# Talking-heads attention, top-1 experts and a dense layer on one core: tokens numbered by partition and tile, one store for the gates, and the low parts of turned operands moved ahead of the maximum

## The chip, the core and the metric

The kernel runs on one core of a Trainium2 chip. The engines of that core named here are TensorE (PE; its weight loads are listed as PEld), VectorE (DVE), ScalarE (ACT), GpSimd (POOL) and SyncE (SP). Each runs its own list of instructions in order and waits at semaphores for the others. Transfers between DRAM and on-chip memory (SBUF) are started from the lists of SP, ACT and POOL and are carried by 16 DMA engines that they share. Matrix products land in PSUM, eight banks of 128 partitions.

The metric is the time of one execution in microseconds of device time. Runs are given as median, lowest and highest. One further execution is taken with a profiler; rows of profile and trace come from that one.

## The reference

Three stages follow one another; the result of each is the input of the next.

```python
# q, k, v: (4, 12, 448, 64)   w_pre, w_post: (12, 12)
scores = scale * q @ k.T                      # per batch and head
scores = einsum('bhij,hg->bgij', scores, w_pre)
attn = exp(scores - max(scores)); attn = attn / (sum(attn) + 1e-09)
attn = einsum('bhij,hg->bgij', attn, w_post)
x = (attn @ v), heads side by side            # (1792, 768)

# experts: emb (8, 768), w1 (8, 768, 1024), w2 (8, 1024, 768)
logits = normalized(x) @ normalized(emb).T / tau
expert_idx = argmax(logits)
gate_w = softmax(logits)[expert_idx]
x = gate_w * (relu(x @ w1[expert_idx]) @ w2[expert_idx])

# dense: w_in (768, 2048), w_out (2048, 768)
h = x @ w_in
out = (h - tanh(h)) @ w_out
```

All inputs and the output are float32. w_in and w_out come as 64-bit floats and are converted on the chip.

## The kernel before

**Precision.** Most products are formed from a high part and a low part of each operand: the high part is the operand copied to a shorter float format (by ScalarE), the low part is the operand minus the high part (by VectorE or POOL). Three products, high by high, low by high and high by low, are summed in PSUM.

**Attention.** Each batch's 448 query rows are cut in four tiles of 120, 120, 120 and 88 rows, 16 tiles T in all (`IT`). A tile is worked in blocks of 10 rows of all 12 heads, so that (row, head) pairs lie on 120 partitions. There are 180 blocks (`NBK`), one for each step of a loop written at lines 1127 to 1160. Step s forms P(s), the product of the rows of S with w_pre (`emit_P`, line 386); VectorE takes the maximum of P from PSUM, ScalarE exponentiates, VectorE makes the weights w from the sum (`emit_W`, lines 402 to 405), and two steps later (`LAG`) TensorE forms T from p and w and ScalarE copies T out (`emit_TE`). The rows of S come from SBUF by a DMA on SP (`emit_relay`), started up to seven steps ahead.

Between these the steps carry the work of other tiles: q and k are turned by TensorE (`tr_q`, `tr_k`) for a later tile, S is formed for the next tile (`emit_S`, `emit_S2`), and A·V and X for an earlier one (`emit_AV2`, `emit_X`). A table (`side`, filled by `at` and `at_e`) says in which step each stands. A turned operand lies in the one PSUM bank with tag e until both its parts are taken: the high part by ScalarE (`flush`, at the start of the next step) and then the low part by VectorE (`flush2`, line 1138, behind `emit_P` and `emit_W` of that step). The next transpose, the second half of `emit_S2` and `emit_X` write the same bank.

The row order inside a block is r, r + nb, r + 2·nb and so on, so position p of a tile is not token p of the tile. The kernel corrects that where rows leave the chip: `x_store` (line 470) writes x to `x_d` in token order through a view of 12 by 10 (or 8 by 10) rows, and the remaining 8 rows of an 88-row tile by a second DMA. `tokf` holds the token number of each place.

**Routing.** `emit_R` ranks the tokens of each expert and makes `ids`, the token numbers of the slots of each expert. Rows of x are then gathered by these numbers from DRAM (`gather`, POOL). The gates, 128 by 16 numbers, are computed in pieces in the first expert (`emit_G`, a generator that `pump(5)` advances after each chunk), written to `gate_d` in token order by 20 DMAs on SP, and gathered again by the same numbers (`gates`, POOL).

**Experts.** Items 0 to 6, an item for overflow rows, and 7 follow one another. An item has eight chunks of h and eight parts of y. During the parts of y of item n the weights of item n+1 are split in high and low parts (`do1`); each split frees one of four buffers, and the load of a later weight is put on SP's queue at that place (`feed1`, `feed2`). At the same place in item 0 the rows of item 1 are multiplied by their gates (line 700) and turned (`xsplit`, line 705). Results go to `yT` in slot order; `sid_d` holds the token number of each slot.

**Dense layer.** Two halves of 896 slots by eight groups g of 256 columns; `stageA` forms h and the activation, `stageB` the product with w_out, one round later. At j = 2 SP loads the token numbers of all slots to `sid`; at the last group of a half POOL scatters the finished rows to the output by them (line 1377).

The scheduler keeps the order that the code is written in, and a DMA on SP or ACT also waits for the DMA eight places before it in a ring of eight semaphores.

Of the kernel before, what the change touches and what calls it, by code (L numbers as in the profile page):

```python
# [9 lines left out]
F32 = mybir.dt.float32  # L10
# [3 lines left out]
I32 = mybir.dt.int32  # L14
# [17 lines left out]
def body(ctx: ExitStack, tc, q, k, v, w_pre, w_post, emb, tau, w1, w2, win, wout, out):  # L32
# [3 lines left out]
    NT = B * S  # L36
# [32 lines left out]
        psum.append(ctx.enter_context(tc.tile_pool(name="psum3", bufs=1, space=PSUM, reuse_waits="tile")))  # L69
        PB.append({"h": 3, "o": 5})  # L70

    x_d = dram.tile([NT, DM], F32, name="x_d")
    NOV = 12
    NTP = NT + CAP
    sid_d = dram.tile([NTP, 1], I32, name="sid_d")
    gate_d = dram.tile([NT, 1], F32, name="gate_d")
    wi_d = dram.tile([DM, F2], F32, name="wi_d")
    wo_d = dram.tile([F2, DM], F32, name="wo_d")

# [58 lines left out]
    if True:  # L138
# [64 lines left out]
        pool.affine_select(tri, tri, pattern=[[1, 128]], compare_op=ALU.is_gt, fill=0.0, base=0, channel_multiplier=-1)  # L203
        revi = cp.tile([128, E], F32, name="revi")
        pool.iota(revi, pattern=[[-1, E]], base=E, channel_multiplier=0, allow_small_or_imprecise_dtypes=True)

        rk = cp.tile([128, 12], F32, name="rk")
        pool.iota(rk[:, 0:11], pattern=[[-10, 11]], base=-10, channel_multiplier=1, allow_small_or_imprecise_dtypes=True)
# [11 lines left out]
        dve.tensor_add(rq[:, 3:4], rq[:, 3:4], rq[:, 5:6])  # L220
        rowf = cp.tile([128, B, 4], F32, name="rowf")
        pool.iota(rowf, pattern=[[S, B], [120, 4]], base=0, channel_multiplier=0, allow_small_or_imprecise_dtypes=True)
        rg4 = tokf.rearrange("p (b t) -> p b t", b=B)
        dve.tensor_scalar(rg4[:, :, 0:3], rowf[:, :, 0:3], rq[:, 1:2], None, ALU.add)
        dve.tensor_scalar(rg4[:, :, 3], rowf[:, :, 3], rq[:, 3:4], None, ALU.add)
        dve.tensor_copy(tokh, tokf)
        pool.iota(iota_s, pattern=[[1, CAP]], base=0, channel_multiplier=0, allow_small_or_imprecise_dtypes=True)

        valid = cp.tile([128, 4], F32, name="valid")
# [156 lines left out]
        def emit_P(i):  # L386
            n = 12 * blocks[i][2]
            t = sr.pop(i)
            pt = ps("b", f"P{i}")
            pe.matmul(pt[:n, :S], wpre[:n, :n], t[:n, :], start=True, stop=True)  # L390
            mx = a2.tile([120, 4], F32, tag="mx", name=f"mx{i}", bufs=5)
            dve.tensor_reduce(mx[:n, 0:1], pt[:n, :S], op=ALU.max, axis=AX.X, negate=True)  # L392
            p = a2.tile([120, S], F32, tag="p", name=f"p{i}", bufs=LAG + 1)
            pj[i] = (p, mx)
            return lambda: act.activation(p[:n, :], pt[:n, :S], AF.Exp, bias=mx[:n, 0:1], scale=1.0, accum_out=mx[:n, 1:2])  # L395
# [72 lines left out]
        xms = {}  # L468

        def x_store(eng, T, xm, cs):  # L470

            b, it = divmod(T, 4)
            i0, n = IT[it]
            r0, nb = b * S + i0, n // 10
            eng.dma_start(x_d[r0:r0 + 10 * nb, cs].rearrange("(m r) d -> r m d", r=nb), xm[:10 * nb, cs])
            if n % 10:
                eng.dma_start(x_d[r0 + 10 * nb:r0 + n, cs], xm[10 * nb:n, cs])

        def emit_X(T, hf, cpy=act.copy):
            b, it = divmod(T, 4)  # L480
# [95 lines left out]
        def emit_G():  # L576
            yield
            bc = lambda t: t.rearrange("p (t o) -> p t o", o=1).to_broadcast([128, 4 * B, E])
            for rn in inv_norm(ssk, 128, 4 * B, "r"):
                yield  # L580
            dve.tensor_sub(lk, lk, bc(mxk))
            yield
            dve.tensor_mul(lk, lk, bc(rn))
            act.activation(lk, lk, AF.Exp)
            yield
            es = small([128, 4 * B], F32, "es")
            dve.reduce_sum(es, lk, axis=AX.X)
            yield
            dve.tensor_scalar_add(es, es, 1e-9)
            yield  # L590
            dve.reciprocal(gate, es)
            yield
            yield

            gvs = dram_disjoint_views(gate_d, 5 * B)
            for T in range(4 * B):
                bq, it = divmod(T, 4)
                i0, n = IT[it]
                r0, nb = bq * S + i0, n // 10
                sp.dma_start(gvs[T][r0:r0 + 10 * nb].rearrange("(m r) o -> r (m o)", r=nb), gate[:10 * nb, T:T + 1])  # L600
                if n % 10:
                    sp.dma_start(gvs[4 * B + bq][r0 + 10 * nb:r0 + n], gate[10 * nb:n, T:T + 1])
                if T % 4 == 3:
                    yield

        def emit_ov():

# [52 lines left out]
    with mctx:  # L660
# [358 lines left out]
        for T in range(4 * B - 1):  # L1019
# [7 lines left out]
            for gi, (_, t1) in enumerate(RG[:-1]):  # L1027
                if t1 == T + 1:
                    for x, y in enumerate((0, 2, 2, 4, 4)):
                        at(e + 5 + y, emit_R, gi, x)  # L1030
        CA = CONV_A
        for j in range(CA):
            st = 12 + (NBK - 24) * j // CA
            at(st - 4, conv_load, j, ap)
            at(st, conv_do, j, ap)
# [41 lines left out]
        def flush2(tag=None):  # L1077
            for x in late2[:]:
                if tag in (None, x[0]):
                    late2.remove(x)  # L1080
                    x[1]()
# [45 lines left out]
        for s in range(NBK + LAG + 6):  # L1127
            todo = side.get(s, [])
            fill = [x for x in todo if x[0] in PEF]
            for fn, a in todo:  # L1130
                if fn in (load_q, load_k, load_v, conv_load):
                    fn(*a)
            flush()
            relay_to(s + NSR - 1)
            ex = emit_P(s) if s < NBK else lambda: None
            if 0 <= s - 1 < NBK:
                emit_W(s - 1)
            flush2()
            for fn, a in todo:
                if fn is emit_R and a[1] in (0, 1, 3):  # L1140
                    fn(*a)
# [120 lines left out]
    with ExitStack() as dctx:  # L1262
# [25 lines left out]
        def wi_load(g, eng=sp):  # L1288
            r = raw6
            eng.dma_start(r, wi_d[:, g * GF * 128:(g + 1) * GF * 128].rearrange("(c p) f -> p c f", p=128))  # L1290
            return r
# [105 lines left out]
        for j, (hf, g) in enumerate(seq):  # L1397
            nx = seq[j + 1][1] if j + 1 < len(seq) else None
            if nx is not None and j:
                wr = wi_load(nx)  # L1400
            if j == 2:
                sp.dma_start(sid, sid_d[0:NT].rearrange("(t p) o -> p (t o)", p=128))

            groups = [(t, nh) for t in range(HT // 128) for nh in range(2)] if prev is not None else []
            work = []
# [72 lines left out]
```

## Time and profile before

| | us |
|---|---|
| median of 3 runs | 1436.76 |
| lowest, highest | 1435.28, 1438.02 |
| the profiled execution | 1437.55 |
| its span, first to last instruction | 1435.8 |
| PE busy in the span | 1317.8 (92%) |
| DVE, ACT, POOL busy | 1030.4 (72%), 751.2 (52%), 531.4 (37%) |

The stages by the time from the span's start: attention steps from 22.9 to about 533 us, the experts from 557 to about 943, the dense layer from there to the end. The mean granted clock of TensorE is 0.97 of full speed.

In the rows further down, "idle before" is the time for which an engine did nothing ahead of an instruction, and the name behind the arrow is what ended that time. Tile names have their numbers left out: P is the score after w_pre, ptk and ptq are turned k and q in PSUM, kh and kl, qh and ql their high and low parts, xgi a gathered block of x, w1hi and w1li the parts of a weight, r a weight as loaded. SPq and ACTq rows are the issuing of DMAs.

### The profile page before, as it was taken

How to read it: one execution, taken by the hardware profiler on the slowest of the kernel's cores; microseconds unless marked ns; L12 is line 12 of the kernel's file. 1: busy time of each engine (PE TensorE's matmuls, PEld its weight loads, DVE VectorE, ACT ScalarE, POOL GpSimd, SP SyncE). 2: the span in 40 equal slices, each digit the busy share in tenths (PEclk: the TensorE clock that was granted, in tenths of full speed). 3: DMA queues.
4: the chain of work that ended last, by engine and by line, in shares of the span. 5: the costliest groups of instructions: out<-in, count | busy, mean ns of one | idle time of the engine just before them, and what ended most of it. 6: DMA issues, size and time to landing. Idle time of an engine off the chain costs nothing. (4 is left out here: it accounts for less than half of the span.)

```text
span 1435.8 us, 25691 instructions
## 1 busy us (share of the span) xinstructions
PE 1317.8 (92%) x9426; PEld 1152.5 (80%) x9426; DVE 1030.4 (72%) x2178; ACT 751.2 (52%) x1515; POOL 531.4 (37%) x528
## 2 busy tenths in 40 slices
PE   8989998999899986488999997969999999999998
PEld 5766776776677766488999996959999998999997
DVE  5766776667667664367777775468888799888886
ACT  6766666665666654224444445256444455544441
POOL 0222322232223223143455442335444446544433
PEclk9999999999999998789999998988999999999999
DMA  5655565556456464458787775222112113122101
GB/s 159 196 154 153 183 191 139 158 185 191 129 170 199 141 206 142 80 169 202 250 252 235 222 219 170 67 67 67 45 44 67 54 57 121 45 67 67 45 23 77
DMA packets 147563, 194.06 MB, mean 135 GB/s; under 512 B 59595, under 2 KB 111227, under 8 KB 147435
## 3 DMA queue, kind: packets, MB, share of 16 engines
q1 hardware_dynamic: 140539, 177.29, 41.9%
q0 software_dynamic: 3024, 12.20, 2.3%
q10 hardware_dynamic: 3872, 2.90, 0.7%
q8 instruction: 76, 1.25, 0.4%
q14 instruction: 52, 0.43, 0.1%
HBM read 130.21 MB, written 23.61 MB: 107 GB/s over the span
## 5 line engine op out<-in xcount | busy, mean ns | idle before, releaser
L427 PEld LDWEIGHTS T<-w,p 120*112 120x112 f32 (+1 forms) x1440 | 165.9, 177 | 65.5 <-issue 49.2
L133 POOL TENSOR_TENSOR cm<-cm,ct 128x256 f32<-128x256 f32 x96 | 73.5, 765 | 335.0 <-DVE ct L130 298.3
L427 PE MATMUL T<-w,p 120*112 120x120 f32 (+1 forms) x1440 | 184.9, 272 | 5.3 <-DVE w L405 3.0
L392 DVE TENSOR_REDUCE mx<-P 120x1 f32<-120x448 f32 x180 | 111.9, 622 | 97.9 <-PE P L390 96.8
L390 PE MATMUL P<-sr,wpre 120*120 120x448 f32 x360 | 166.5, 544 | 1.0 <-DMA sr<-ssb 0.9
L395 ACT ACTIVATE p<-P,mx 120x448 f32<-120x448 f32 x180 | 113.8, 632 | 97.1 <-DVE mx L402 86.1
L1317 POOL TENSOR_TENSOR gl<-th,gh 128x448 fp32r<-128x448 f32 x64 | 74.8, 1169 | 239.3 <-ACT gh L1316 192.7
L1331 PE MATMUL h<-yh,wih 128*128 128x448 f32 x384 | 142.7, 372 | 11.1 <-ACT yh L1279 9.2
L1368 PE MATMUL o<-woh,gh 128*128 128x384 f32 x448 | 150.7, 336 | 1.8 <-DVE acc L1374 1.8
L1369 PE MATMUL o<-wol,gh 128*128 128x384 f32 x448 | 150.8, 337 | 0.0
L1370 PE MATMUL o<-woh,gl 128*128 128x384 f32 x448 | 150.7, 336 | 0.0
L1333 PE MATMUL h<-yh,wil 128*128 128x448 f32 x384 | 143.2, 373 | 3.1 <-POOL wil L1306 3.1
L1332 PE MATMUL h<-yT,wih 128*128 128x448 f32 x384 | 142.7, 372 | 0.4 <-DVE yT L1280 0.4
L1374 DVE TENSOR_TENSOR acc<-acc,o 128x384 f32<-128x384 f32 x196 | 106.5, 547 | 45.6 <-PE o L1370 45.1
L1337 ACT ACTIVATE u<-h 128x448 f32<-128x448 f32 x64 | 34.9, 545 | 183.8 <-PE h L1333 183.8
L785 PE MATMUL hi<-xhi,w1hi 128*128 128x256 f32 x384 | 111.5, 290 | 15.4 <-DVE hli L789 15.2
L432 ACT COPY A<-T 112x480 f32<-112x480 f32 x180 | 101.2, 562 | 21.9 <-PE T L427 21.5
L727 PE MATMUL ypi<-hhi,w2hi 128*128 128x256 f32 x384 | 111.9, 291 | 0.0
L729 PE MATMUL ypi<-hhi,w2li 128*128 128x256 f32 x384 | 110.0, 286 | 0.0
L786 PE MATMUL hi<-xli,w1hi 128*128 128x256 f32 x384 | 109.9, 286 | 0.0
L728 PE MATMUL ypi<-hli,w2hi 128*128 128x256 f32 x384 | 109.8, 286 | 0.0
L787 PE MATMUL hi<-xhi,w1li 128*128 128x256 f32 x384 | 109.5, 285 | 0.0
(259 smaller groups left out, 3398.2 us busy)
## 6 DMA issues: line engine op xcount, KB each, us to landing
sr<-ssb SPq DMA_DIRECT2D x176, 210.0 KB
r<-in_moe_w SPq DMA_DIRECT2D x72, 384.0 KB
r<-in_moe_w SPq DMA_DIRECT2D x52, 512.0 KB
craw<-in_moe_w_in SPq DMA_DIRECT2D x48, 256.0 KB
craw<-in_moe_w_out SPq DMA_DIRECT2D x48, 256.0 KB
raw<-wi_d SPq DMA_DIRECT2D x15, 768.0 KB
wor<-wo_d SPq DMA_DIRECT2D x15, 768.0 KB
wi_d<-cm SPq DMA_DIRECT2D x48, 128.0 KB
```

What stands on the lines that cost most here:

```text
L390: pe.matmul(pt[:n, :S], wpre[:n, :n], t[:n, :], start=True, stop=True)
L392: dve.tensor_reduce(mx[:n, 0:1], pt[:n, :S], op=ALU.max, axis=AX.X, negate=True)
L395: return lambda: act.activation(p[:n, :], pt[:n, :S], AF.Exp, bias=mx[:n, 0:1], scale=1.0, accum_out=mx[:n, 1:2])
L427: pe.matmul(pt[:CP, c * n:(c + 1) * n] if m == 10 else pv[:, c], p[:n, c * CP:(c + 1) * CP], w[:n, :] if m == 10 else wv, start=True, stop ...
L727: pe.matmul(o, wh[:, sl], a, start=False, stop=False)
L785: pe.matmul(pt[:, :256], wh[:, sl], xh[:, c, :], start=c == 0, stop=False)
L1331: pe.matmul(pt[:, :S], wi[0][:, c, sl], yh[:, c, :], start=c == 0, stop=False)
L1332: pe.matmul(pt[:, :S], wi[0][:, c, sl], yl[:, c, :], start=False, stop=False)
L1333: pe.matmul(pt[:, :S], wi[1][:, c, sl], yh[:, c, :], start=False, stop=c == KD - 1)
L1368: pe.matmul(pt[:, :384], gh[:, sl], wo[0][:, f, n0:n0 + 384], start=f == 0, stop=False)
L1369: pe.matmul(pt[:, :384], gh[:, sl], wo[1][:, f, n0:n0 + 384], start=False, stop=False)
L1370: pe.matmul(pt[:, :384], gl[:, sl], wo[0][:, f, n0:n0 + 384], start=False, stop=f == GF - 1)
```

## The change

Tokens are numbered p·16 + T by partition p and tile T, which needs 2048 numbers for 1792 tokens. `x_d` and `gate_d` have 2048 rows in this numbering, `tokf` is an iota, and each store of x is one DMA with one row for each partition. The 256 rows that belong to no token are written with zeros by five DMAs in step 8, and a table `row_d` from number to token row by a sixth. All gates are stored by one DMA on ACT's queue, 64 bytes for each partition. In the dense layer the numbers of the slots go to `sidc`, and POOL looks the token rows up in `row_d` by 14 gathers at j = 3 to 7. And `flush2`, the low parts, is called inside `emit_P`, behind the product and ahead of the maximum.

```diff
+    NC = 128 * 4 * B
+    x_d = dram.tile([NC, DM], F32, name="x_d")
+    row_d = dram.tile([NC, 1], I32, name="row_d")
...
+        pool.iota(tokf, pattern=[[1, 4 * B]], base=0, channel_multiplier=4 * B, allow_small_or_imprecise_dtypes=True)
+        dve.tensor_copy(tokh, tokf)
...
+        def store_rows():
+            zr = xbuf[1]
+            dve.memset(zr, 0.0)
+            xv = x_d.rearrange("(p t) d -> t p d", t=4 * B)
+            sp.dma_start(x_d[NC - 128:NC, :], zr)
+            for b in range(B):
+                sp.dma_start(xv[4 * b + 3, 88:120, :], zr[:32])
+            sp.dma_start(row_d.rearrange("(p t) o -> p (t o)", t=4 * B), rowi)
...
             pe.matmul(pt[:n, :S], wpre[:n, :n], t[:n, :], start=True, stop=True)
+
+            flush2()
             mx = a2.tile([120, 4], F32, tag="mx", name=f"mx{i}", bufs=5)
...
-            eng.dma_start(x_d[r0:r0 + 10 * nb, cs].rearrange("(m r) d -> r m d", r=nb), xm[:10 * nb, cs])
-            if n % 10:
-                eng.dma_start(x_d[r0 + 10 * nb:r0 + n, cs], xm[10 * nb:n, cs])
+            n = IT[T % 4][1]
+            eng.dma_start(x_d.rearrange("(p t) d -> t p d", t=4 * B)[T, :n, cs], xm[:n, cs])
...
-            for T in range(4 * B):
...
-                sp.dma_start(gvs[T][r0:r0 + 10 * nb].rearrange("(m r) o -> r (m o)", r=nb), gate[:10 * nb, T:T + 1])
-                if n % 10:
-                    sp.dma_start(gvs[4 * B + bq][r0 + 10 * nb:r0 + n], gate[10 * nb:n, T:T + 1])
-                if T % 4 == 3:
-                    yield
+            act.dma_start(gate_d.rearrange("(p t) o -> p (t o)", t=4 * B), gate)
+            yield
...
+        at(8, store_rows)
...
-            flush2()
...
+            if 2 < j < 8:
+                for k in range(3 * (j - 3), min(NT // 128, 3 * (j - 2))):
+                    pool.indirect_dma_start(out=sid[:, k:k + 1], out_offset=None, in_=row_d,
+                                            in_offset=bass.IndirectOffsetOnAxis(ap=sidc[:, k:k + 1], axis=0))
             if j == 2:
-                sp.dma_start(sid, sid_d[0:NT].rearrange("(t p) o -> p (t o)", p=128))
+                sidc = dp.tile([128, NT // 128], I32, name="sidc")
+                sp.dma_start(sidc, sid_d[0:NT].rearrange("(t p) o -> p (t o)", p=128))
```

Three places show what stands where. VectorE in attention step 28, before: mx is the maximum of P and, in the next three rows, the steps to the weights w of the block before; kl1_3 is the low part of turned k (batch 1, pair 3), lg a small sum of X.

```order
L392 TENSOR_REDUCE mx28_1283<-P28_1281 120x1
L402 TENSOR_SCALAR mx27_1237<-mx27_1237 120x1
L403 RECIPROCAL mx27_1237<-mx27_1237 120x1
L405 TENSOR_SCALAR w27_1288<-wpost_130,mx27_1237 120x120
L311 TENSOR_TENSOR kl1_3_1277<-ptk1_3_1271,kh1_3_1276 128x448
L493 TENSOR_REDUCE lg_174<-X0_0_1298 120x8
```

The same place in the changed kernel:

```order
L325 TENSOR_TENSOR kl1_3_1287<-ptk1_3_1281,kh1_3_1286 128x448
L408 TENSOR_REDUCE mx28_1294<-P28_1291 120x1
L418 TENSOR_SCALAR mx27_1248<-mx27_1248 120x1
L419 RECIPROCAL mx27_1248<-mx27_1248 120x1
L421 TENSOR_SCALAR w27_1299<-wpost_131,mx27_1248 120x120
L504 TENSOR_REDUCE lg_177<-X0_0_1308 120x8
```

The low part of k has moved ahead of the maximum and the three steps of the weights.

SP's queue in the first expert, before: the last seven of its rows around the end of the gate stores, with the first loads behind them (r2_1 and r1_1 are weights of expert 1).

```order
L600 DMA gate_d_65<-gate_77 12x10x1 x3
L600 DMA gate_d_65<-gate_77 8x10x1
L602 DMA gate_d_65<-gate_77 8x1
L941 DMA r2_1_0_7396<-in_moe_w2 128x768
L935 DMA r1_1_4_7402<-in_moe_w1 128x1024
L935 DMA r1_1_5_7408<-in_moe_w1 128x1024
L941 DMA r2_1_1_7432<-in_moe_w2 128x768
```

The same place in the changed kernel, from the last load for expert 0 on:

```order
L943 DMA r2_0_7_7234<-in_moe_w2 128x768
L943 DMA r2_1_0_7385<-in_moe_w2 128x768
L937 DMA r1_1_4_7391<-in_moe_w1 128x1024
L937 DMA r1_1_5_7397<-in_moe_w1 128x1024
L943 DMA r2_1_1_7421<-in_moe_w2 128x768
```

All stores of gates have left this queue, and the loads for expert 1 follow directly on those for expert 0.

POOL in the dense layer at j = 3, before: gl is the low part of the activation, wol the low part of a block of w_out.

```order
L1317 TENSOR_TENSOR gl0_2_0_12241<-th_12397,gh0_2_0_12240 128x448
L1317 TENSOR_TENSOR gl0_2_1_12243<-th_12460,gh0_2_1_12242 128x448
L1306 TENSOR_TENSOR wol3_12510<-wor3_12506,woh3_12509 128x768
L1317 TENSOR_TENSOR gl0_3_0_12514<-th_12538,gh0_3_0_12513 128x448
L1306 TENSOR_TENSOR wol3_12510<-wor3_12506,woh3_12509 128x768
```

And in the changed kernel:

```order
L1319 TENSOR_TENSOR gl0_2_0_12228<-th_12384,gh0_2_0_12227 128x448
L1405 DMA sid_70<-row_d_64,sidc_12221 128x1 x3
L1319 TENSOR_TENSOR gl0_2_1_12230<-th_12447,gh0_2_1_12229 128x448
L1308 TENSOR_TENSOR wol3_12500<-wor3_12493,woh3_12499 128x768
L1319 TENSOR_TENSOR gl0_3_0_12504<-th_12528,gh0_3_0_12503 128x448
```

Three lookups stand between two low parts of the activation of the group before; the others stand at the same place of the next four rounds, three each and two in the last.

## Rows read from the trace of the kernel before

**Rows 1.** Windows: length; PE, PEld, DVE, ACT, POOL busy (instructions); clock; DMA share; GB/s.

```profile
300.00:350.00 50.00, 47.04 (x405) 34.27 (x405) 37.43 (x119) 31.06 (x74) 15.52 (x22) 1.00 0.62 190
...
1100.00:1150.00 50.00, 50.00 (x269) 48.21 (x268) 40.83 (x63) 25.49 (x47) 22.10 (x15) 1.00 0.20 64
```

**Rows 2.** Waits of PE, 0 to 560 us: us in total, times, longest.

```profile
PE S L347 <- DVE kl L311: 8.3, 9, 0.9
PE ptk L304 <- PE T L427: 4.5, 5, 1.0
PE X L488 <- DVE ql L328: 3.9, 4, 1.0
PE X L488 <- DVE kl L311: 3.7, 3, 1.5
...
PE ptk L304 <- issue: 1.7, 1, 1.7
```

**Rows 3.** Timeline: start, us, engine, line, operation [idle before]; PE, then ACT, then DVE.

```profile
92.29 0.98 PE L427 MATMUL T<-w,p 120*112 120x120 f32 x8
94.37 0.93 PE L488 MATMUL X<-ien,xT 128*120 128x136 f32 x6 [1.10 <-DVE kl L311]
...
91.81 0.53 ACT L310 CAST kh<-ptk 128x448 fp32r<-128x448 f32 x1
...
92.49 0.62 DVE L392 TENSOR_REDUCE mx<-P 120x1 f32<-120x448 f32 x1 [1.52 <-PE P L390]
...
93.61 0.62 DVE L311 TENSOR_TENSOR kl<-ptk,kh 128x448 fp32r<-128x448 f32 x1
```

**Rows 4.** Timeline of PE, around 84 us.

```profile
83.98 0.41 PE L347 MATMUL S<-kh,qh 64*88 64x448 f32 x1 [0.94 <-DVE kl L311]
```

**Rows 5.** Groups on DVE, 30 to 535 us: count, busy, mean ns, idle before.

```profile
L328 DVE TENSOR_TENSOR ql<-ptq,qh 128x360 fp32r<-128x360 f32 (+1 forms) x28 | 13.9, 496 | 0.0
L311 DVE TENSOR_TENSOR kl<-ptk,kh 128x448 fp32r<-128x448 f32 x18 | 11.1, 617 | 0.0
```

**Rows 6.** Waits of PE, 560 to 950 us.

```profile
PE xti L709 <- DVE xgi L700: 30.1, 2, 21.0
```

**Rows 7.** Timeline of SP's queue, first expert.

```profile
576.02 3.04 SPq L600 DMA_DIRECT2D gate_d<-gate  x4
...
595.07 0.47 SPq L602 DMA_DIRECT2D gate_d<-gate  x1
...
596.12 0.84 SPq L935 DMA_DIRECT2D r<-in_moe_w  x2
```

**Rows 8.** Timeline of DVE, then ACT, then PE, first expert.

```profile
585.54 2.36 DVE L685 TENSOR_TENSOR w1li<-r,w1hi 128x1024 fp32r<-128x1024 f32 x2
...
590.96 0.95 DVE L685 TENSOR_TENSOR w2li<-r,w2hi 128x768 fp32r<-128x768 f32 x1
...
608.10 1.05 ACT L683 CAST w1hi<-r 128x1024 fp32r<-128x1024 f32 x1 [18.27 <-DMA r<-in_moe_w]
609.56 1.04 ACT L683 CAST w1hi<-r 128x1024 fp32r<-128x1024 f32 x1 [0.42 <-DMA r<-in_moe_w]
...
613.41 1.51 PE L709 MATMUL xti<-ident,xgi 128*128 128x128 f32 x6 [21.02 <-DVE xgi L700]
```

**Rows 9.** Window with the gap in the first expert.

```profile
600.00:604.00 4.00, 0.00 (x0) 0.00 (x0) 0.00 (x0) 0.00 (x0) 0.00 (x0) 0.50 0.91 43
```

**Rows 10.** Timeline of SP, then ACT, one expert later.

```profile
656.11 1.46 SPq L935 DMA_DIRECT2D r<-in_moe_w  x2
...
663.83 1.05 ACT L683 CAST w1hi<-r 128x1024 fp32r<-128x1024 f32 x1 [0.67 <-DMA r<-in_moe_w]
```

**Rows 11.** Timeline of POOL in the dense layer.

```profile
1008.20 1.15 POOL L1317 TENSOR_TENSOR gl<-th,gh 128x448 fp32r<-128x448 f32 x1 [6.69 <-ACT gh L1316]
...
1202.38 0.96 POOL L1377 DMA_INDIRECT out<-acc,sid  x1 [0.30 <-DVE acc L1374]
```

**Rows 12.** Timeline of POOL at the end of attention.

```profile
553.01 1.18 POOL L690 DMA_INDIRECT xgi<-x_d,ids  x1 [8.40 <-issue]
```

More of the change, by code (lines that the diff above doesn't have):

```diff
@@ L70, in ps_dense @@
         PB.append({"h": 3, "o": 5})
-    x_d = dram.tile([NT, DM], F32, name="x_d")
+    NC = 128 * 4 * B
+    x_d = dram.tile([NC, DM], F32, name="x_d")
+    row_d = dram.tile([NC, 1], I32, name="row_d")
     NOV = 12
@@ L75, in body @@
     sid_d = dram.tile([NTP, 1], I32, name="sid_d")
-    gate_d = dram.tile([NT, 1], F32, name="gate_d")
+    gate_d = dram.tile([NC, 1], F32, name="gate_d")
     wi_d = dram.tile([DM, F2], F32, name="wi_d")
@@ L222, in body @@
         pool.iota(rowf, pattern=[[S, B], [120, 4]], base=0, channel_multiplier=0, allow_small_or_imprecise_dtypes=True)
-        rg4 = tokf.rearrange("p (b t) -> p b t", b=B)
+        rowi = cp.tile([128, 4 * B], I32, name="rowi")
+        rg4 = rowi.rearrange("p (b t) -> p b t", b=B)
         dve.tensor_scalar(rg4[:, :, 0:3], rowf[:, :, 0:3], rq[:, 1:2], None, ALU.add)
         dve.tensor_scalar(rg4[:, :, 3], rowf[:, :, 3], rq[:, 3:4], None, ALU.add)
-        dve.tensor_copy(tokh, tokf)
+        def store_rows():
[6 more added lines that the diff above has]
+            sp.dma_start(row_d.rearrange("(p t) o -> p (t o)", t=4 * B), rowi)
         pool.iota(iota_s, pattern=[[1, CAP]], base=0, channel_multiplier=0, allow_small_or_imprecise_dtypes=True)
@@ L470, in x_store @@
         def x_store(eng, T, xm, cs):
-            b, it = divmod(T, 4)
-            i0, n = IT[it]
-            r0, nb = b * S + i0, n // 10
-            eng.dma_start(x_d[r0:r0 + 10 * nb, cs].rearrange("(m r) d -> r m d", r=nb), xm[:10 * nb, cs])
-            if n % 10:
-                eng.dma_start(x_d[r0 + 10 * nb:r0 + n, cs], xm[10 * nb:n, cs])
+            n = IT[T % 4][1]
+            eng.dma_start(x_d.rearrange("(p t) d -> t p d", t=4 * B)[T, :n, cs], xm[:n, cs])
         def emit_X(T, hf, cpy=act.copy):
@@ L593, in emit_G @@
             yield
-            gvs = dram_disjoint_views(gate_d, 5 * B)
-            for T in range(4 * B):
-                bq, it = divmod(T, 4)
-                i0, n = IT[it]
-                r0, nb = bq * S + i0, n // 10
-                sp.dma_start(gvs[T][r0:r0 + 10 * nb].rearrange("(m r) o -> r (m o)", r=nb), gate[:10 * nb, T:T + 1])
-                if n % 10:
-                    sp.dma_start(gvs[4 * B + bq][r0 + 10 * nb:r0 + n], gate[10 * nb:n, T:T + 1])
-                if T % 4 == 3:
-                    yield
+            act.dma_start(gate_d.rearrange("(p t) o -> p (t o)", t=4 * B), gate)
+            yield
         def emit_ov():
@@ L1130, in body @@
             for fn, a in todo:
-                if fn in (load_q, load_k, load_v, conv_load):
+                if fn in (load_q, load_k, load_v, conv_load, store_rows):
                     fn(*a)
```

## The prediction

> **What bounds the kernel now.** I read the busy time by stretch first, to see which engine sets the pace in each stage; then the list of who waited for whom, kept to TensorE, in each stage; then the rows in order of time around the two largest kinds of wait; last the engines that the change gives work to. In the attention stage TensorE is busy for 47 of 50 us, VectorE for 37, ScalarE for 31; in the dense layer TensorE is busy all 50 us and POOL 22 [rows 1]. So a microsecond in which TensorE does nothing is a microsecond of the program, and work on the other engines counts only where TensorE waits for it.
>
> In the attention stage nearly all of TensorE's idle time has one cause. The waits are 8.3 us (S for the low part of k), 4.5 and 1.7 us (a transpose of k), 3.9 and 3.7 us (X for the low part of q or k), 22.1 us in all [rows 2]. The 4.5 us are booked on T, which had run just ahead on the same engine, and 1.7 us on nothing; but these transposes write the PSUM bank, one buffer, that the low part before them still reads, so I count them too. One such place shows how it comes about: T ends about 93.27 and X could start; the high part of k was copied at 91.81 to 92.34 on ScalarE; but VectorE first takes the maximum of P (92.49), then three steps for the weights, and only at 93.61 to 94.23 the low part that frees the bank; X starts at 94.37, 1.10 us late [rows 3].
>
> The largest single wait is in the first expert: 21.0 of 30.1 us of waiting for the rows times their gate [rows 6], a gap that ends at 613.41 [rows 8]. Two things end late there. The gates reach DRAM through 20 stores on SP's queue, from 576.02 to past 595.07 [rows 7]; and the loads of the next expert's weights stand behind them in that queue. The buffer for the first of these (tile 4 of expert 1) is free when tile 0 has been split, half-way through the pair that starts at 585.54, at 585.54 + 1.18 = 586.7 [rows 8]; its load starts at 596.12 [rows 7] and is used at 608.10, the next at 609.56 [rows 8]. Meanwhile the DMA engines are 0.91 busy at only 43 GB/s [rows 9], which fits 1792 single gates of 4 bytes draining ahead of the loads.
>
> **The change part by part.** The sum is made against the profiled execution, 1437.55 us (span 1435.8), 0.8 above the median of the runs.
>
> *Low part ahead of the maximum.* The low part can start when the high part is there: 92.34 in [rows 3], so it ends at 92.34 + 0.62 = 92.96 instead of 94.23, ahead of the end of T (93.27), and the 1.10 us go. What it costs: the maximum, queued behind it on VectorE, starts at about 92.96 instead of 92.49, 0.47 us later, and with it exp on ScalarE, the copy of T behind exp, and the weights w. T of this step uses p and w of two steps before and P the other of two banks, so a step of slack covers it; where S is evacuated ahead of exp, ScalarE is not at exp yet. Without that cover it is 0.5 us a step. One kind keeps a part: S at 83.98 [rows 4] follows on a k that was turned in the step before, behind a low part of q; there the copy of the high part stands on ScalarE behind the exp that is now late. Six of the nine S waits are of that kind, and I leave each 0.5 us: 22.1 − 6 × 0.5 = 19.1 us gained. Ends: 22.1, and 10 if the late maximum gives half back.
>
> *One store for all gates, on ScalarE's queue.* The 20 stores leave SP; one of 128 runs of 64 bytes stands on ScalarE behind the copy of a weight and ahead of an evacuation of h. I price its issue by the row of the stores that it replaces with the same kind of instruction, 3.04/4 = 0.76 us [rows 7], half of it hidden by ScalarE's own waits for h: 0.4 us lost (ends 0 and 0.8). The next expert's load starts at 586.7 instead of 596.12. When does it land? One expert later the same pair, issued from 656.11, the second at about 656.11 + 1.46 − 0.33 = 657.24, has its second used at 663.83 [rows 10], 6.6 us later. The second of our pair then starts at 586.7 + 1.2 + 6.6 = 594.5 instead of 609.56, and from there to TensorE's start it was 613.41 − 609.56 = 3.85: 598.4. Gain 15.0 us. Upper end: VectorE has its last split until 590.96 + 0.95 = 591.9, then two splits of 1.18 and one of 0.95 [rows 8] stand ahead of the product with the gates, so not before 595.2: 18.2 us. Lower end: only the start moves, the landing still takes 12 us: 596.12 − 586.7 = 9.4. I take 15.0, the row of the same transfer. What is next there: some 6 us of idle time remain, behind VectorE's splits, and the clock, at 1.2 GHz (0.50) in the gap [rows 9], I take to be low at the restart as now. The gathers of gates, which waited for the last store, come 20 us early and are no longer near the end. Behind this point the order on all engines is as before, so the stages behind it shift as a whole.
>
> *Numbering.* Rows of x go to p·16 + t; a store is one DMA where it was one or two, the bytes are the same. At the end of attention ScalarE issues two stores instead of four; POOL's first gather stands 8.40 us idle for them and the slots and starts at 553.01 [rows 12]. The last small store goes, by the price of a store above 0.7 us (ends 0 and 1.5). The new stores of zero rows and of the row table (6 on SP in step 8, 0.79 MB, behind a memset on VectorE that holds up one maximum) stand ahead of the copies of S rows for steps 15 and up, which are issued seven steps ahead; 180 steps take some 510 us, 2.8 each, so some 20 us cover about 5 us of issue and 4 us of transfer. Nothing; without that cover 5 us. The table of overflow rows is computed three small VectorE steps earlier: nothing, ends −1 and +1.
>
> *Lookups in the dense layer.* 14 gathers of 128 numbers on POOL in five groups of at most three. A POOL DMA in this stage takes 0.96 us [rows 11], with the gap of 0.30 ahead of it about 1.25, so a group takes 3.75 us. Each stands behind one split of g and ahead of another, where POOL is idle 6.69 us [rows 11]: hidden. The scatters read the result a whole half later. SP's load that feeds them blocks no one.
>
> The same row bears on a rule. The Trainium skill (SBUF — State Buffer, section "SBUF: two separate sides") says that a DMA issued from GpSimd stalls while VectorE runs certain fast copies, because its descriptors can't be written. It would make a group longer than its gap, rival (d); its own example is 620 ns grown to 3100 ns. In [rows 11] a scatter took 0.96 us with VectorE busy for 41 of 50 us [rows 1].
>
> Sum: 1437.55 − 19.1 − 15.0 − 0.7 + 0.4 = 1403.2; less the 0.8 to the median, **1402.4 us**.
>
> **The rivals.** (a) *The weights land late anyway*: the 12 us are the loads' own and not the gates in front of them. For it: two loads of 0.5 MB are a lot of bytes; against it: 43 GB/s in that time [rows 9]. Gain 9.4 for 15.0: 1408. (b) *The stall moves to the late maximum*: exp, the copy of T and the next high part all slip by 0.5 us and half of the gain goes (10 for 19.1): 1411.5. For it: ScalarE waits for the maximum in most steps; against it: the slack of a step. (c) *Everything goes*: 22.1, 18.2 and 1.5 with no cost on ScalarE: 1395.0. (d) *POOL's lookups are held up by VectorE*. If each took three times 1.25 us, a group would take 11.25 us in a gap of 6.69, 4.6 late; five times that is 23 us if TensorE waited for every one, and half of it, 11.5, since g is read only a round later: 1414. The scatter in [rows 11] speaks against it. The Trainium skill's rule above (SBUF — State Buffer, section "SBUF: two separate sides") is this mechanism. (e) *The change does not do what it says*: the low part waits for ScalarE's copy and starts no earlier. Then 19.1 are lost: 1421.5. Against it, 92.34 lies ahead of 92.49 [rows 3]. (f) *Slower*: the chain maximum, exp, copy of T, high part becomes the pace of the attention stage, and each moved low part adds its full time: 18 of k and 28 of q, 11.1 + 13.9 = 25.0 us [rows 5], and each of the 22.1 us comes back as a wait for T's copy; with only 9.4 from the gates and 5 us for the zero rows: 1436.8 + 25.0 − 9.4 + 0.4 + 5 = 1458. It decides where TensorE's slack behind the maximum is under 0.5 us a step; what speaks for and against it is what does for (b), and it needs all of it.
>
> **How the numbers follow.** Forecast 0.50 (1402), (a) 0.18, (b) 0.14, (c) 0.08, (d) 0.03, (e) 0.02, (f) 0.05 (0.01 of it in a weak form that ends level). Range: (c) 1395.0 with 2 us for the unknown sides of the small terms, and up past (b) and (d), (a) and (b) together being 1417: 1393 to 1419. About 0.2% (3 us) is what a measurement can tell here. Faster 0.95, within 0.2% 0.01 (a weak form of (f)), slower 0.04.
>
> **What would show it.** In the profile after: the waits of S, X and transposes for low parts fall from 22 us to about 3; the maximum starts 0.5 us later behind a low part, and no wait of T for w or of P for p grows by more than 1 or 2 us. The gap ahead of the first product with gates falls from 21.0 to about 6, no store of gates on SP, the next weights issued within 1 us of their buffer. POOL's lookups take about 1 us each, and TensorE stays at 50 of 50 us in the dense layer. Wrong would be: the gap stays above 11 us (a), the attention stage gains under 12 us (b, e), or new waits for g or for the weights' low parts appear in the dense layer (d).

## The result, and the profile after

| | before | changed |
|---|---|---|
| median of 4 runs, us | 1436.02 | 1398.67 |
| lowest, highest | 1433.13, 1438.02 | 1395.92, 1402.23 |
| the profiled execution, its span | 1437.55, 1435.8 | 1396.13, 1394.4 |
| PE busy in the span | 1317.8 (92%) | 1310.2 (94%) |

The ratio is 0.9743 (95% interval 0.971 to 0.9776): 37 us faster. The two profiled executions lie 41.4 us apart, more than the medians: the one of before is above its median and the one after below.

First the attention steps, as windows over them (length; busy time of PE, PEld, DVE, ACT, POOL with their instructions; clock; DMA share; GB/s), from 25 us to just before `ids`, the slot numbers, which end the stage. Before:

```profile
25.00:551.00 526.00, 492.98 (x4274) 364.51 (x4272) 359.49 (x1125) 332.84 (x783) 151.67 (x198) 1.00 0.57 171
```

and changed:

```profile
25.00:528.00 503.00, 489.01 (x4274) 363.37 (x4274) 356.39 (x1125) 328.83 (x784) 152.04 (x198) 1.00 0.62 181
```

TensorE's idle time falls from 526 − 493 = 33 to 503 − 489 = 14 us, and its busy time, over equally many matmuls (4274), by 4. What is left of the waits of [rows 2] in the changed kernel, from 0 to 528 us:

```profile
PE T L443 <- DVE w L421: 3.0, 2, 2.2
PE S L361 <- DVE kl L325: 2.8, 7, 0.5
...
PE ptk L318 <- DVE ql L342: 1.3, 3, 0.8
...
PE T L443 <- ACT A L448: 1.0, 2, 0.5
```

S for kl is down from 8.3 to 2.8 us, no wait of X is left, and the transposes keep 1.3. T for w has its 3.0 us as before; the 1.0 us of T for A, the copy of an earlier T, is new. The place of [rows 3], in the changed kernel, PE, then ACT, then DVE:

```profile
91.04 0.98 PE L443 MATMUL T<-w,p 120*112 120x120 f32 x8
91.86 0.90 PE L499 MATMUL X<-ien,xT 128*120 128x136 f32 x6
...
90.56 0.53 ACT L324 CAST kh<-ptk 128x448 fp32r<-128x448 f32 x1
...
91.12 0.62 DVE L325 TENSOR_TENSOR kl<-ptk,kh 128x448 fp32r<-128x448 f32 x1 [1.69 <-ACT kh L324]
91.66 0.61 DVE L408 TENSOR_REDUCE mx<-P 120x1 f32<-120x448 f32 x1
```

The low part starts 0.03 us after its high part and is done at 91.74; X follows T without a gap, where it stood idle for 1.10 us.

Then the first expert, to be held against [rows 7, 8]: SP, then ACT, then DVE, then PE in the changed kernel.

```profile
563.60 1.46 SPq L937 DMA_DIRECT2D r<-in_moe_w  x2
...
568.47 1.05 ACT L685 CAST w1hi<-r 128x1024 fp32r<-128x1024 f32 x1 [1.84 <-DMA r<-in_moe_w]
570.02 1.04 ACT L685 CAST w1hi<-r 128x1024 fp32r<-128x1024 f32 x1 [0.50 <-DMA r<-in_moe_w]
...
573.11 1.14 DVE L702 TENSOR_SCALAR xgi<-xgi,gxi 128x768 f32<-128x768 f32 x2
...
573.87 1.06 PE L711 MATMUL xti<-ident,xgi 128*128 128x128 f32 x6 [4.66 <-DVE xgi L702]
```

The next expert's weights are issued at 563.60, at once when their buffer is free (the split on VectorE that frees it ends near 563.53), the second is used at 570.02, and the gap ahead of the first product with gates is 4.66 us where it was 21.02. In the window while they land, against [rows 9], the DMA engines are as busy but carry eight times the bytes:

```profile
568.00:572.00 4.00, 1.21 (x11) 1.00 (x9) 2.84 (x3) 2.82 (x3) 0.00 (x0) 1.00 0.95 346
```

From there to the first product of the dense layer it is 330.8 us after (573.87 to 904.65) and 330.7 before (613.41 to 944.06), and the dense layer shifts as a whole. In it TensorE is still busy for 50 of 50 us, with POOL at 25 where it was at 22 [rows 1]:

```profile
1060.00:1110.00 50.00, 50.00 (x269) 48.20 (x268) 40.85 (x63) 25.50 (x48) 25.32 (x18) 1.00 0.20 64
```

So the 41.4 us of the profiled pair come 22.8 from attention (`ids` at 528.30 for 551.14), 0.8 from the first gathers of x, 15.9 from the first expert (to 573.87 for 613.41, 39.5 in all), 0.4 from small waits up to the middle of the dense layer, and 1.4 from how long the last scatter runs after the last sum.

### The profile page after: what moved, and what is told of

The parts are those of the page before. It is cut to its first block, busy times and chain, and to the rows that moved or that the text cites. A ratio compares the mean times of both kernels' runs of the same rounds, so it can differ in the third digit from the quotient of the medians.

```text
span 1394.4 us, 25678 instructions
## 1 busy us (share of the span) xinstructions
PE 1310.2 (94%) x9426; PEld 1146.0 (82%) x9426; DVE 1027.0 (74%) x2179; ACT 746.7 (54%) x1515; POOL 545.9 (39%) x543
## 2 busy tenths in 40 slices
DMA packets 146646, 194.87 MB, mean 140 GB/s; under 512 B 58422, under 2 KB 110054, under 8 KB 146518
## 3 DMA queue, kind: packets, MB, share of 16 engines
q8 instruction: 76, 1.25, 0.4%
```

## The experiments

Three groups of kernels ran beside the kernel before. Its median was 1432.67 in the first, 1430.80 in the second and 1433.11 in the third, so kernels are compared by their ratio to it, or directly inside a group. The changed kernel ran again in the second.

| kernel | median | ratio to before (95%) |
|---|---|---|
| low parts alone | 1412.51 | 0.9850 (0.9831 to 0.9869) |
| changed, low parts back | 1417.71 | 0.9892 (0.9874 to 0.9909) |
| low parts behind the maximum | 1405.39 | 0.9813 (0.9795 to 0.9831) |
| one gate store on SP | 1396.79 | 0.9750 (0.9733 to 0.9767) |
| changed kernel again | 1395.04 | 0.9744 (0.9724 to 0.9764) |
| 16 column stores on POOL | 1407.84 | 0.9839 (0.9823 to 0.9855) |
| 16 column stores on SP | 1397.42 | 0.9761 (0.9742 to 0.9780) |
| product with gates earlier | 1387.61 | 0.9703 (0.9687 to 0.9720) |
| the old 20 stores | 1408.65 | 0.9839 (0.9809 to 0.9870) |
| 16 stores to neighbours | 1405.92 | 0.9821 (0.9798 to 0.9843) |
| 14 lookups in one group | 1401.80 | 0.9791 (0.9765 to 0.9818) |
| product with gates first | 1381.06 | 0.9633 (0.9611 to 0.9655) |

**The two halves apart.** The kernel before with `flush2()` moved alone:

```diff
             pe.matmul(pt[:n, :S], wpre[:n, :n], t[:n, :], start=True, stop=True)
+            flush2()
...
                 emit_W(s - 1)
-            flush2()
```

> The kernel before with the low parts alone moved ahead of the maximum; numbering, gate stores and dense layer as before. Theory 1 (the low part only had to start when its high part was there; each wait that goes also gives back the overlap of neighbouring matmuls): the attention steps shorten by 23 us, as between the two traces (waits of TensorE there from 33 to 14 us, its busy time from 493 to 489), and nothing else moves: 1436.0 - 23 = 1413. Theory 2 (only the waits of rows 2 count, as the prediction has it): 1436.0 - 19.1 = 1417. Rival (part of the gain in attention comes from the numbering, its fewer stores and shorter tables): under 12 us, 1424 or more.

and the changed kernel with this edit undone.

> The changed kernel with the low parts put back behind the maximum and the weights w. Theory 1: the 23 us of the attention steps come back and the gate part stays: 1398.7 + 23 = 1422; the two parts add up, so this kernel and the one with the low parts alone together gain what the change gains. Theory 2: 1398.7 + 19.1 = 1418. If the two parts overlap (an earlier end of attention meeting a transfer that is late anyway), this kernel lies under 1415.

The first gains 20 us by the medians and 1.5%, 21.5 us, by the ratio; the second 15.0 and 1.1%, 15.5 us. Together that is 35 to 37, what the change gains: the halves add up. Attention itself shows it at the last maximum of P (VectorE, 180 in each kernel), which stands at 532.55 us before; in the kernel with the low parts alone:

```profile
510.94 0.61 DVE L394 TENSOR_REDUCE mx<-P 96x1 f32<-96x448 f32 x1
```

and in the changed kernel with them back:

```profile
531.00 0.61 DVE L406 TENSOR_REDUCE mx<-P 96x1 f32<-96x448 f32 x1
```

In the changed kernel it is 510.96. So the low parts are worth 21.6 us up to here from one side and 20.0 from the other, between the 19.1 and the 23 that the two theories had. Part of the 4 us of busy time is something else, the clock (below).

**Half-way.** The changed kernel with the low parts between the maximum and the weights w:

```diff
-            flush2()
             mx = a2.tile([120, 4], F32, tag="mx", name=f"mx{i}", bufs=5)
             dve.tensor_reduce(mx[:n, 0:1], pt[:n, :S], op=ALU.max, axis=AX.X, negate=True)
+            flush2()
```

> The changed kernel with the low parts between the maximum and the three steps to the weights w: the maximum is as early as before the change, the low part 0.5 us later than in the changed kernel and 0.6 us earlier than in the kernel before. Theory (the low part frees the bank, and the maximum has slack): of some 25 waits of 0.9 us about 0.5 us each are left, so 25 x 0.5 = 12 us more than the changed kernel at most, and more likely 6 to 10 since some transposes come later than that: 1405 to 1409. Rival (the late maximum gives back part of the gain, so that this place is the better one): 1398 or less.

1405.39 against 1396.79 for the kernel with one store on SP in the same group, which has the low parts where the change puts them: 8.6 us lost, as the theory had it (6.1 between the two profiled executions). The early maximum gives next to nothing back: T's waits for w stay at 3.0 us and those for A go from 1.0 to 0.4. Its slack covers the half microsecond. The waits of TensorE from 0 to 536 us name mx at line 417 as releaser, the first step to the weights, which writes into the same tile as the maximum; it is the low part just ahead of it on VectorE that frees the bank:

```profile
PE S L361 <- DVE mx L417: 3.5, 9, 0.5
PE X L498 <- DVE mx L417: 3.2, 7, 0.5
...
PE ptk L318 <- PE T L442: 2.3, 6, 0.7
```

The sixteen waits on S and X are 0.42 us on average and 0.5 at most, a little less than one maximum (0.61).

**Which queue.** The changed kernel with its one store on SP (`act.dma_start` to `sp.dma_start`).

> The changed kernel with its one store of all gates on SP's queue in place of ScalarE's. Theory (what cost time was the number of stores and of 4-byte pieces, not the queue): one issue of 0.3 us on SP at about 550 to 563 us, the next expert's weights still issued near 563.6, gap ahead of the first product with gates 4.7 us: 1398.7 within 1.5. Rival (the queue counts: the store holds SP until the gates are there, or the loads wait behind it): the gap grows by 3 us or more, 1402 or more.

1396.79, a ratio of 0.9750 against 0.9743 and 0.9744: the queue makes no difference that can be measured, so long as there is one store.

**Many stores, and their addresses.** Sixteen stores of 128 single gates on POOL, then on SP, each gate 64 bytes from the next in DRAM:

```diff
-            act.dma_start(gate_d.rearrange("(p t) o -> p (t o)", t=4 * B), gate)
+            gvs = dram_disjoint_views(gate_d, 4 * B)
+            for T in range(4 * B):
+                sp.dma_start(gvs[T].rearrange("(p t) o -> t p o", t=4 * B)[T], gate[:, T:T + 1])
```

> The changed kernel with its one store of all gates replaced by 16 stores of 128 single gates of 4 bytes, on POOL's queue, which has nothing else there: SP's queue stays free, the 2048 pieces of 4 bytes are back. Theory 1 (of the 16 us gained, some 9 were SP's queue and some 7 the single gates draining ahead of the loads): the weights are issued near 563.6 as in the changed kernel but land about 6 us later, so 6 us over the changed kernel. Theory 2 (only SP's queue counted, the late landing was something else): within 1.5 us of the changed kernel.

> The changed kernel with its one store replaced by 16 stores of 128 single gates of 4 bytes, on SP's queue ahead of the next expert's loads. Theory 1: SP issues them from 550 to about 566 to 570 (0.76 us each, more where it waits for the store eight places before), the next loads follow 3 to 8 us late and land late too: 9 to 15 us over the changed kernel, most of the gate part given back. Theory 2 (the 20 stores cost because of their 12 x 10 order, not their number or size): within 3 us of the changed kernel.

On POOL they cost 12.8 us, but not by the loads, which landed in the usual time (issued 574.79, first use 579.16). The 16 issues took 8.58 us on POOL, and an iota for the overflow tables stood behind them; VectorE waited 10.7 us for it, and TensorE 9.4 for VectorE. The run says nothing about the single gates: the expectation took POOL's queue for empty, and the trace has only 368 DMA packets more than that of the changed kernel (147014 and 146646), where the same stores on SP add 2160 (148806), so on POOL the gates are not on record as single pieces. On SP they took 8.51 us, were through before the loads, and cost 2.4 us by the medians, inside the spread of the runs. Theory 1 fell: neither sixteen stores nor pieces of 4 bytes account for 15 us by themselves.

What is left is where the pieces go. The old stores, and sixteen whose gates are neighbours in DRAM:

```diff
-                sp.dma_start(gvs[T].rearrange("(p t) o -> t p o", t=4 * B)[T], gate[:, T:T + 1])
+                sp.dma_start(gvs[T].rearrange("(t p) o -> t p o", p=128)[T], gate[:, T:T + 1])
```

> The changed kernel with the 20 gate stores of the kernel before, in their 12 x 10 order, on SP and spread over four pieces as there; everything else as changed. (The gates land under the old numbers and are read under the new ones, so tokens are weighted with other tokens' gates; the 256 numbers in between are filled by one small store in step 8.) Theory 3 (the gate part of the change is the form of these stores and nothing else of the change): the gap ahead of the first product with gates is back at some 19 to 21 us, 14 to 17 us over the changed kernel. Rival (with the columns on SP costing only 2.4 us, the cost of before came from elsewhere, such as the numbering or the queue's older loads): under 6 us over the changed kernel.

> The changed kernel with 16 stores of 128 single gates on SP, as in the run with columns on SP, but each to 128 neighbouring numbers in DRAM (4 bytes apart instead of 64). (The gates land under tile-major numbers and are read under the new ones, so tokens are weighted with other tokens' gates.) Theory 3a (single gates that are neighbours in DRAM are slow to store, whatever their order): the stores take 15 to 20 us on SP instead of 8.5 and the gap is back, 10 us or more over the changed kernel. Theory 3b (the 12 x 10 order of the old stores is what is slow, neighbours in themselves are not): within 4 us of the changed kernel, as with the columns 64 bytes apart.

The old stores bring most of it back: by the ratio 0.0095 × 1433 = 14 us over the changed kernel, with a gap of 19.51 us. The neighbours cost 0.0077 × 1433 = 11 us, with a gap of 14.34: theory 3a. With the old stores, SP's queue, the first gather of gates on POOL, the first use on ACT and the first product with gates:

```profile
572.84 0.98 SPq L946 DMA_DIRECT2D r<-in_moe_w  x2
...
579.21 0.97 POOL L710 DMA_INDIRECT gxi<-gate_d,ids  x1 [26.47 <-DMA gate_d<-gate]
...
583.50 1.04 ACT L694 CAST w1hi<-r 128x1024 fp32r<-128x1024 f32 x1 [16.69 <-DMA r<-in_moe_w]
...
588.89 1.52 PE L720 MATMUL xti<-ident,xgi 128*128 128x128 f32 x6 [19.51 <-DVE xgi L711]
```

SP's queue in the run with pieces 64 bytes apart, then the first use on ACT:

```profile
553.20 8.51 SPq L607 DMA_DIRECT2D gate_d<-gate  x16
563.30 0.33 SPq L945 DMA_DIRECT2D r<-in_moe_w  x1
564.51 1.46 SPq L939 DMA_DIRECT2D r<-in_moe_w  x2
...
568.85 1.05 ACT L687 CAST w1hi<-r 128x1024 fp32r<-128x1024 f32 x1 [1.31 <-DMA r<-in_moe_w]
```

and with neighbours, SP's queue, POOL's first gather, the first uses on ACT and the first product with gates:

```profile
553.05 14.48 SPq L607 DMA_DIRECT2D gate_d<-gate  x16
567.94 0.33 SPq L945 DMA_DIRECT2D r<-in_moe_w  x1
570.79 1.16 SPq L939 DMA_DIRECT2D r<-in_moe_w  x2
...
577.54 0.97 POOL L703 DMA_INDIRECT gxi<-gate_d,ids  x1 [24.73 <-DMA r<-in_moe_w]
...
579.18 1.04 ACT L687 CAST w1hi<-r 128x1024 fp32r<-128x1024 f32 x1 [11.78 <-DMA r<-in_moe_w]
580.47 1.05 ACT L687 CAST w1hi<-r 128x1024 fp32r<-128x1024 f32 x1 [0.24 <-DMA r<-in_moe_w]
...
584.32 1.51 PE L713 MATMUL xti<-ident,xgi 128*128 128x128 f32 x6 [14.34 <-DVE xgi L704]
```

with this window while the loads are on their way, and these two waits of SP's queue:

```profile
572.00:576.00 4.00, 0.00 (x0) 0.00 (x0) 0.00 (x0) 0.00 (x0) 0.00 (x0) 0.50 0.95 57
...
SPq L607 <- DMA gate_d<-gate: 4.0, 1, 4.0
...
SPq L939 <- DMA gate_d<-gate: 2.9, 2, 2.5
```

Same number, same size, same queue, and the same 148806 packets. The stores hold SP for 14.48 us instead of 8.51, not because an issue is dearer (the median is 0.43 us in both) but mostly because SP waits for earlier stores of gates to land, 4.0 us; with 64 bytes between the pieces it never does. The gates themselves land late: POOL's first gather of them starts 563.80 − 561.71 = 2.1 us after the last issue has ended with 64 bytes, and 577.54 − 567.53 = 10.0 us with neighbours (its row names a load, but of what SP sends the gather needs the gates alone). And the loads behind them are used 579.18 − 570.79 = 8.4 us after their issue, where the run with 64 bytes has 568.85 − 564.51 = 4.3 and the changed kernel 568.47 − 563.60 = 4.9. With the old stores it is 583.50 − 572.84 = 10.7 us.

**Lookups.** All 14 at j = 3:

```diff
-            if 2 < j < 8:
-                for k in range(3 * (j - 3), min(NT // 128, 3 * (j - 2))):
+            if j == 3:
+                for k in range(NT // 128):
```

> The changed kernel with all 14 lookups of the dense layer in one group at j = 3 instead of five groups of at most three. Theory (a group is hidden as long as it fits POOL's idle time of some 6.7 us between two low parts; one of 14 x 1.4 = 19.6 us does not): POOL is some 13 us late once, low parts of g and of the next weights come late, and TensorE waits 5 to 12 us: 5 to 12 us over the changed kernel. Rival (a round of slack hides that too): within 2 us.

6.7 us by the ratio, 0.0047 × 1433, one wait of which shows (TensorE, 985 to 1030 us):

```profile
PE o L1372 <- POOL gl L1319: 4.7, 1, 4.7
```

**What is left of the gap.** In the first expert and in the overflow item the product with the gates stood behind all six weight splits, and the last two of these wait for loads. First it was moved ahead of these two, then ahead of all, with the turnings behind the second split:

```diff
...
                 if n == 0 or e == OV:
-                    todo += gx[1]
-                todo += [lambda j=j, t=t, hf=hf: xsplit(nx, t, j, hf, f"i{n + 1}") for j, t in enumerate(nxg) for hf in range(2)]
+                    todo = todo[:4] + gx[1] + xs + todo[4:]
+                else:
+                    todo += xs
```

```diff
-                    todo = todo[:4] + gx[1] + xs + todo[4:]
+                    todo = gx[1] + todo[:2] + xs + todo[2:]
```

(`todo` holds the six splits, `gx[1]` the products, and `xs`, set in a line left out here, the four turnings of the old second line.)

> The changed kernel with, in the first expert and in the overflow item, the product with the gates and the turning of the rows moved ahead of the last two weight splits of the next item (they stood behind all six). Theory (what is left of the gap, 4.7 us in the first expert and 9.1 us in the overflow item, is waiting for those two weights' loads and splits, on which the product does not depend): the gaps fall to about 1 and 2 us, and TensorE does the turning and the rest of y in that time: some 10 us under the changed kernel, 36 + 10 = 46 us under the kernel before. Rival (the next item's first h needs those weights anyway and waits for them instead): the stall moves there, 0 to 3 us gained.

> The version with the gates' product moved ahead of the last two weight splits, taken further: the product first, then two splits, then all four turnings, then the other four splits. Theory (its remaining gaps of 2.3 us in the first expert and 5.7 us in the overflow item are still waits for the product behind the four splits; in the overflow item the last split sets the end, 2 us earlier): 3 to 5 us under the version before it, some 11 to 12 us under the changed kernel. Rival (the delayed splits delay the loads behind them, and h of the next item waits for these): no gain over that version or slower.

The first is 7.4 us under the changed kernel of its group: the waits for the product fell from 13.5 us (two, 9.1 the longer) to 8.0 (5.7 and 2.3), not to 3. The second stands at 0.9633, 0.0111 × 1433 = 15.9 us under the changed kernel by the ratio (14.0 by the medians, from two groups). Under the first it is some 10 us by the ratio, but 5 to 16 by the two intervals and 3.9 between the two profiled executions; whether that is more than the 3 to 5 expected is not shown. In its overflow item the product hardly shows (TensorE, 800 to 850 us), and in the first expert not at all:

```profile
PE xti L711 <- DVE xli L715: 2.8, 1, 2.8
PE yti L775 <- DVE yi L771: 1.1, 1, 1.1
PE yti L775 <- ACT yi L770: 0.9, 1, 0.9
PE hqi L812 <- ACT hsi L807: 0.7, 1, 0.7
PE xti L711 <- DVE xgi L702: 0.4, 1, 0.4
```

This version is faster than both kernels, 1381.06 against 1433.11 for the kernel before.

## Why the prediction held, point by point

**Low parts.** Predicted 19.1 us, with ends of 10 and 22.1; measured 20 to 21.6 with nothing else changed. The mechanism is as it was read: the low part could start when its high part was there (0.03 us after it), and the maximum had a step's slack. The terms inside the sum came out too: the S waits keep 2.8 us for the 3.0 that 6 × 0.5 had, with 0.5 as the longest. The 22.1 us left out 1.5 of the same kind, S and a transpose behind a low part of q in the kernel before:

```profile
PE S L347 <- DVE ql L328: 1.0, 2, 0.7
...
PE ptk L304 <- DVE ql L328: 0.5, 1, 0.5
```

With these, the waits for low parts and for A went from 25 (23.6 us) to 12 (5.1 us): 18.5 us. What the sum left out altogether is that TensorE's busy time falls too. Up to a wait for w near the end of attention, with the clock at 1.00, before and changed:

```profile
25.00:530.02 505.02, 478.43 (x4090) 351.77 (x4088) 348.27 (x1087) 324.46 (x766) 142.72 (x195) 1.00 0.58 173
...
25.00:508.42 483.42, 476.03 (x4090) 352.09 (x4090) 345.24 (x1088) 320.44 (x767) 143.08 (x195) 1.00 0.63 182
```

That is 2.4 us; the rest of the 4.0 is the slower clock behind that wait (below), 1.6 in the longer AV row. The low parts alone take 3.1 us off the busy time of before (475.31, with two matmuls fewer on record), and the changed kernel has 1.4 less than with them back (477.39), so 0.1 to 0.24 us for each of the 13 waits that went. That a wait also costs the overlap of the matmuls around it is argued, not tested by itself.

**Gate store.** Predicted 15.0 us, with ends of 9.4 and 18.2, and 15.3 with the small terms (+ 0.7 − 0.4); measured 15.0 to 15.5 with the low parts back, where the small terms are in, and 15.9 for the first expert of the profiled pair. Its two steps were a start 9.4 us earlier and a landing of 6.6 us instead of 12. The start is as said, 0.07 us after the buffer. The landing is 568.47 − 563.60 = 4.9 us for the first, and for the second 570.02 − (563.60 + 1.46 − 0.33) = 5.3. One expert later, where I had taken it from, it is 6.6 us in the changed kernel too (622.54 − 615.89), so the row was read rightly, but the first expert is faster than that place. The remaining gap is 4.66 us for the 6 expected. The runs with neighbours and with the old stores confirm that the late landing was the gates in front of the loads, so rival (a), 1408, falls. What I gave as its cause was too general, though: "single gates of 4 bytes" 64 bytes apart cost next to nothing. And "draining ahead of the loads" is not what the packet records of the trace show: in the kernel before nearly all pieces are on record by 596.5, at some 9 ns each, and in the gap it is packets of the loads themselves (3072 bytes, 0.12 us as a rule) that take up to 5.6 us.

**End of attention and the small terms.** The first product on turned x gains 0.8 us on `ids`, for 0.7. The issue on ScalarE took 0.33 us instead of 0.76, and on SP instead of ScalarE nothing changed. A wait of 0.8 us of h for the overflow tables is new, as the tables come three steps earlier, inside the ±1. The zero rows and the row table took SP 40.57 to 44.37 us, and the waits of P for S rows stay at 1.0 us for 0.9: nothing, as said.

**Lookups.** The 14 took 1.10 us each in the median, for 0.96, and no engine waited for them; a group takes 3.8 us. Rival (d) needed 11 us for a group. In one group of 18 us they cost 6.7 us in all, so the cover that the prediction named, POOL's idle time between two low parts, is real, and it is used up between 3.8 and 18 us.

**Other rivals.** (b) and (f) rested on the maximum. The run with the low part behind it gained at most 0.6 us from an earlier maximum and lost 8.6, and T's waits for w are unchanged. (e) falls with the first row of DVE above. (c), 1395.0, is as near to the result as the forecast: of its terms attention came close (20 to 21.6 of 22.1), the gates did not (15.0 to 15.9 of 18.2). 1402.4 against 1398.67 is 3.7 us too high: 0.7 in the median of the kernel before (1436.76 in the sum, 1436.02 beside the result), about 1 to 2.5 in the low parts and up to 1 in the landing. What is left can't be told apart: the interval of the result is 32 to 42 us, and the clock, for which the sum had no term, moves 1 to 3 from one execution to the next.

## What to carry to other kernels

A step that frees a shared buffer belongs on its engine as soon as its input is there, ahead of work that has slack, and the price of the move can be read as waits that end on that step; the gain is a little more than those waits. When loads behind a string of small stores are late, count the queue's time and the landing time apart, and look at the addresses before the number of stores: gates stored as whole 64-byte rows cost one issue, single gates 64 bytes apart nothing that could be measured, and gates scattered to neighbouring words 11 to 14 us. And when a wait ends on an in-order engine, ask whether what it waits for depends on what stands ahead of it there: here that question, put to what was left of the gap, gave another 14 to 16 us.

## What the runs showed of the hardware

*Neighbouring words in DRAM.* 128 pieces of 4 bytes that lie 4 bytes apart take longer to land than 64 bytes apart: 16 such stores held SP for 14.48 instead of 8.51 us, and the gates could be gathered 10.0 instead of 2.1 us after the last issue. In the packet records the pieces look alike, 9 ns each in both runs. From 572 to 576 us hardly one is left, and the 0.95 busy at 57 GB/s are nearly all packets of the loads, 3072 bytes, which take up to 4.1 us where 0.12 is the rule. Why neighbouring words hold up what stands behind them stays open. The Trainium skill (DMA: Bandwidth & Descriptors, section "Why small descriptors are slow (HBM only)") gives a fixed cost for each small piece; by that alone the two would be equal, and the measurement decides here.

*The clock near the end of attention.* There TensorE waits 2.16 or 2.17 us for w in every kernel. In some executions its clock was then granted at 0.5 for a few microseconds, the lower of its two levels (1.2 and 2.4 GHz), in others not. The window in the kernel with the low parts alone:

```profile
512.00:514.00 2.00, 2.00 (x19) 1.78 (x19) 1.93 (x5) 0.94 (x3) 1.45 (x1) 0.50 0.53 209
```

and at the same place in the changed kernel:

```profile
512.00:514.00 2.00, 1.71 (x30) 1.48 (x27) 1.93 (x5) 1.20 (x4) 1.47 (x1) 1.00 0.51 197
```

32 matmuls of AV took 3.47 us there and 1.86 here. From the last maximum to `ids` it is 18.59 us before, 20.06 with the low parts alone and 17.34 in the changed kernel, with the same work. The changed kernel, run again, had the slow stretch too:

```profile
510.24 1.05 PE L443 MATMUL T<-w,p 120*112 120x120 f32 x8 [2.16 <-DVE w L421]
511.21 3.47 PE L461 MATMUL AV<-A,v 112*64 112x120 f32 x32
```

So it differs from one execution of the same kernel to the next, and the 1 to 3 us that it moves belong to neither half of the change. The Trainium skill (TensorE: Matmul & The Clock Gate, Part 1) says that the moment at which the clock changes varies from run to run; the two executions of the changed kernel agree with it.

*Gathers beside weight splits.* Where sixteen column stores on SP moved the gathers of gates into the weight splits, three took 1.53, 1.67 and 1.97 us on POOL, and the fourth, behind them, 0.94:

```profile
563.80 1.53 POOL L703 DMA_INDIRECT gxi<-gate_d,ids  x1 [10.84 <-issue]
565.63 1.67 POOL L703 DMA_INDIRECT gxi<-gate_d,ids  x1 [0.30 <-issue]
567.61 1.97 POOL L703 DMA_INDIRECT gxi<-gate_d,ids  x1 [0.30 <-issue]
569.88 0.94 POOL L703 DMA_INDIRECT gxi<-gate_d,ids  x1 [0.30 <-issue]
```

VectorE was busy for 5.89 us of the 6.20 from 563.80 to 570.00. That is the direction of rival (d), at up to twice the time where it took three times; it was not tested by itself. In the dense layer the lookups took 0.94 to 1.25 us.
